# Grouping the query projections of an attention-and-FFN kernel into bursts of eight heads

## The chip, the cores and the metric

The kernel runs on one core of a Trainium2 chip. The metric is the device time of one execution, in microseconds. A profile of one more execution was taken beside the timed runs; its instructions carry start times, so a reader can follow each engine. In the rows PE is TensorE (PEld its weight loads), DVE is VectorE, ACT is ScalarE, POOL is GpSimd and SP is the engine that issues most transfers.

## The reference

One block computes `x + s * silu(ffn)` from a layer-normed input `xn` of 2048 rows by 448 columns.

- Attention `s`: `q = xn @ wq` gives 16 query heads of 256 columns; there are 8 key/value heads, each shared by two neighbouring query heads. Only the last 512 keys of the cache are used (W = 512). Per head: scores `q k^T / 16`, softmax over 512 keys, times `v`; the 16 heads side by side (4096 columns) go through `wo` (4096 x 448).
- FFN: `(gelu(xn @ w_gate) * (xn @ w_up)) @ w_down` with 1792 hidden columns, then silu.

All inputs and the output are bf16.

## The kernel before

The rows are cut into 4 chunks of 512 (`NQC`), each of 4 tiles of 128 (`TPC`). First comes the FFN, chunk by chunk (`gate_up`, `down`); the last chunk's `down` is interleaved into the start of attention. Its result stays in SBUF as `gy`.

Attention is one loop over 64 steps `i` (4 chunks times 16 heads), each with four tiles `t`. The order in which TensorE gets its work is written out by hand in that loop:

- `scores(i, t)`: two matmuls (L420) into PSUM bank 4 or 5 in turn; ScalarE takes the exponential with a row sum (L424) into a ring of bf16 tiles `pr`; VectorE takes the reciprocal (L426) and scales the tile (L427); SP issues a transposing transfer into `pT[i % 4]` (issued at L236). The ring has 9 tiles.
- `values(i, e_)`: four matmuls (L440) of `V` with the transposed head, one group for each half `e_` of the 256 columns, at even `t`. VectorE casts the result into `oT` (L446; ScalarE does so for the last two heads, L448). The PSUM banks come from a list of eight, `(0, 6, 0, 6, 0, 1, 6, 6)`, walked group by group; it is lined up so that heads 3, 7, 11, ... use bank 6 for both groups.
- `outproj(G, t, part)`: four heads `G` of one row tile times `wo`, eight matmuls (L460), half of them at `t` = 1 and half at `t` = 3. VectorE adds the result into `acc` (L481). After a chunk's last group POOL multiplies by `gy` and adds the x tile `xr` (L485, L487) and the chunk is stored.
- `q_burst(G)`: the query projections of four heads, 56 matmuls (L406). The contraction is 448 = 7 x 64, so a matmul uses 64 of the 128 rows of the array and two run side by side. ScalarE copies the result into `qT` (L410), two heads at a time, through banks 0 to 3. A burst comes at `t` = 0 of every fourth head, right behind that slot's value group.
- `silu(n)`: a tanh on ScalarE (L499) and two products on POOL (L500, L502), for one of 16 row tiles, behind heads 7, 10, 13, ...

Values trail the scores: the first group runs at head 2, tile 2, so a head's two groups run two heads later at `t` = 2 and three heads later at `t` = 0. Output groups begin at head 6. Behind the loop stand what is left of values and output groups, in the order of a string (`"vvovovv"`, v for values, o for an output group), and the last four output tiles.

Every engine's list of operations is in the program's order, and a small recorder (`Rec`) puts in a semaphore wait where an operation reads or rewrites what another engine or a transfer holds. Buffers of attention lie over those of the FFN, which are dead by then.

Of the kernel before, what the change touches and what calls it, by code (L numbers as in the profile page):

```python
# [5 lines left out]
ACT = mybir.ActivationFunctionType  # L6
ALU = mybir.AluOpType
BF16 = mybir.dt.bfloat16
# [3 lines left out]
P = 128  # L12
# [129 lines left out]
def bass_recurrent_scan__sliding_block_cached__geglu_ffn__prompt_kernel(nc, A_x, A_k, A_v, A_wq, A_wo, B_x, B_wg, B_wu, B_wd, out):  # L142
    _, S, D = A_x.shape
    Hkv, Sk, Dh = A_k.shape[1], A_k.shape[2], A_k.shape[3]
    HD = A_wq.shape[1]
    Hq = HD // Dh
# [4 lines left out]
    NT = NQC * TPC  # L151
# [7 lines left out]
    with es:  # L159
        off = [16512]  # L160

        def sb(name, shape, dt, at=None):
            n = 4 if dt == F32 else 2
            for x in shape[1:]:
                n *= x
            if at is None:
                at = off[0]
                off[0] += (n + 31) // 32 * 32
            return R.place(name, shape, dt, at), at + (n + 31) // 32 * 32
# [24 lines left out]
        hb, ffn_end = sb("hb", [P, NHB, QC], BF16)  # L194


        NPT = 4
        qT, at = sb("qT", [P, 6, NE, QC], BF16, gu_at)
        oT = [None, None]
        oT[0], at = sb("oT0", [P, 4 * NE, QC], BF16, at)  # L200
        xr, at = sb("xr", [P, TPC, D], BF16, at)
        assert at <= x_at
        pT, at = sb("pT", [P, NPT, NJ, QC], BF16, x_at)
        pr = []
        while at + 2 * W <= d_at:
            t_, at = sb("pr%d" % len(pr), [P, W], BF16, at)
            pr.append(t_)
        at = hb_at
        while at + 2 * W <= ffn_end:
            t_, at = sb("pr%d" % len(pr), [P, W], BF16, at)  # L210
            pr.append(t_)
        NPR = len(pr)
        oT[1], at = sb("oT1", [P, 4 * NE, QC], BF16, d_at)
        acc, at = sb("acc", [P, TPC, D], F32, at)
        tmp, at = sb("tmp", [P, 2, D], F32, at)
        ofin, at = sb("ofin", [P, TPC, D], BF16, at)
        assert at <= hb_at, (at, hb_at)
# [175 lines left out]
        NI = NQC * Hq  # L393
        NG = NI // 4

        def q_burst(G):

            c, h0 = divmod(4 * G, Hq)
            for n in range(4):
                hp, e_ = divmod(n, 2)  # L400
                s, i = 2 * (n % 2) if G else (4, 0, 2, 0)[n], (4 * G + 2 * hp) % 6

                def run(e, hp=hp, e_=e_, s=s):
                    for k in range(NK):
                        for b, lo in ((s, 0), (s + 1, HP)):
                            ins = e.matmul(bank(b), lhsT=wq[lo:lo + HP, k, h0 // 2 + hp, e_ * P:(e_ + 1) * P],  # L406
                                           rhs=xnT[lo:lo + HP, c, k, :], start=k == 0, stop=k == NK - 1)
                    return ins
                pe(run, r=xn(c) + [("wq", lo, k) for lo in range(2) for k in range(NK)], w=[("ps", s), ("ps", s + 1)])
                act(lambda e, e_=e_, s=s, i=i: e.activation(  # L410
                    qT[:, i:i + 2, e_, :], psum[:, s * 512:(s + 2) * 512].rearrange("p (a q) -> p a q", a=2), ACT.Copy),
                    r=[("ps", s), ("ps", s + 1)], w=[("qT", i, e_), ("qT", i + 1, e_)])

        def scores(i, t):
            g, n = (i % Hq) // 2, i * TPC + t
            b, s = 4 + n % 2, n % NPR

            def run(e):
                for k in range(NE):
                    ins = e.matmul(bank(b), lhsT=qT[:, i % 6, k, t * P:(t + 1) * P], rhs=kT[:, g, k, :],  # L420
                                   start=k == 0, stop=k == NE - 1)
                return ins
            pe(run, r=[("kT", g), ("qT", i % 6, 0), ("qT", i % 6, 1)], w=[("ps", b)])
            act(lambda e: e.activation(pr[s][:, :], bank(b), ACT.Exp, scale=scale, accum_out=den[:, s:s + 1]),  # L424
                r=[("ps", b)], w=[("pr%d" % s,), ("den", s)])
            dve(lambda e: e.reciprocal(rden[:, s:s + 1], den[:, s:s + 1]), r=[("den", s)], w=[("rden", s)])  # L426
            dve(lambda e: e.tensor_scalar(pr[s][:, :], pr[s][:, :], rden[:, s:s + 1], None, op0=ALU.mult),  # L427
                r=[("pr%d" % s,), ("rden", s)], w=[("pr%d" % s,)])
            dmaT(pT[:, i % NPT, :, t * P:(t + 1) * P], pr[s][:, :], r=[("pr%d" % s,)], w=[("pT", i % NPT, t)], lane="p%d" % s)

        def values(i, e_):
            g = (i % Hq) // 2
            idx = (i % 4) * NE + e_
            at = 2 * i + e_ + 5

            b = (0, 6, 0, 6, 0, 1, 6, 6)[at % 8] if at < 2 * NI else (0, 6, 0, 6, 1)[at - 2 * NI]

            def run(e):
                for j in range(NJ):
                    ins = e.matmul(bank(b), lhsT=V[:, j, g, e_ * P:(e_ + 1) * P], rhs=pT[:, i % NPT, j, :],  # L440
                                   start=j == 0, stop=j == NJ - 1)
                return ins
            pe(run, r=[("pT", i % NPT, t) for t in range(TPC)] + [("V", j) for j in range(NJ)], w=[("ps", b)])
            dst, key = oT[(i // 4) % 2][:, idx, :], ("oT%d" % ((i // 4) % 2), idx)
            if i < NI - 2:
                dve(lambda e: e.tensor_copy(dst, bank(b)), r=[("ps", b)], w=[key])  # L446
            else:
                act(lambda e: e.activation(dst, bank(b), ACT.Copy), r=[("ps", b)], w=[key])  # L448

        def outproj(G, t, part, half=None):  # L450

            n8 = 4 * NE
            lo, hi = (0, D) if half is None else (half * D // 2, (half + 1) * D // 2)
            b = ((2, 2), (3, 5), (7, 4), (0, 6))[t][half or 0] if G == NG - 1 else (7, 7, 7, 4)[t] if G == NG - 2 else 7
            c, h0 = divmod(4 * G, Hq)
            end = c == NQC - 1

# [10 lines left out]
            if end and h0 == Hq - 4:  # L468
                dve(lambda e: e.tensor_tensor(tmp[:, t % 2, lo:hi], bank(b, D)[:, lo:hi], gy[:, n, lo:hi], ALU.mult),  # L469
                    r=[("ps", b), ("gy", n)], w=[("tmp", t % 2)])  # L470
                dve(lambda e: e.tensor_tensor(ofin[:, t, lo:hi], tmp[:, t % 2, lo:hi], acc[:, t, lo:hi], ALU.add),  # L471
                    r=[("tmp", t % 2), ("acc", t)], w=[("ofin", t, lo)])
                if t == TPC - 1:
                    dma("sync" if half else "scalar", o_view[:, c, t, lo:hi], ofin[:, t, lo:hi], r=[("ofin", t, lo)])
                elif half != 0:
                    dma("sync", o_view[:, c, t, :], ofin[:, t, :], r=[("ofin", t, 0), ("ofin", t, lo)])
                return
            if h0 == 0:
                dve(lambda e: e.tensor_copy(acc[:, t, :], bank(b, D)), r=[("ps", b)], w=[("acc", t)])
# [1 line left out]
                dve(lambda e: e.tensor_tensor(acc[:, t, :], bank(b, D), acc[:, t, :], ALU.add),  # L481
                    r=[("ps", b), ("acc", t)], w=[("acc", t)])
            if h0 == Hq - 4 or end and h0 == Hq - 8:
                dst, key = (acc, ("acc", t)) if end else (ofin, ("ofin", t))
                pool(lambda e: e.tensor_tensor(tmp[:, t % 2, :], acc[:, t, :], gy[:, n, :], ALU.mult),  # L485
                     r=[("acc", t), ("gy", n)], w=[("tmp", t % 2)])
                pool(lambda e: e.tensor_tensor(dst[:, t, :], tmp[:, t % 2, :], xr[:, t, :], ALU.add),  # L487
                     r=[("tmp", t % 2), ("xr",)], w=[key])
                if t == TPC - 1 and not end:
                    dma("gpsimd", o_view[:, c, :, :], ofin[:, :, :], r=[("ofin", t) for t in range(TPC)])  # L490
                    load_xr(c + 1)

        def load_xr(c):
            dma("gpsimd", xr[:, :, :], x_view[:, c, :, :], w=[("xr",)])

        def silu(n):

# [26 lines left out]
        q_burst(0)  # L524
        load_xr(0)

        fill = {}
# [5 lines left out]
        for i in range(NI):  # L533
            for t in range(TPC):
                scores(i, t)
                if 4 * i + t in fill:
                    down(NQC - 1, *fill[4 * i + t])
                if t % 2 == 0 and 4 * i + t >= 10:
                    values(*pv.pop(0))
                if 6 <= i and t % 2:  # L540
                    outproj(*outs[0], range(2 * t - 2, 2 * t + 2))
                    if t == TPC - 1:
                        outs.pop(0)
                if t == 0 and i % 4 == 3 and i + 1 < NI:
                    q_burst(i // 4 + 1)
            if 7 <= i and (i - 7) % 3 == 0 and (i - 7) // 3 < NT:
                silu((i - 7) // 3)

        for what in "vvovovv":
            if what == "v":  # L550
                values(*pv.pop(0))
            else:
                outproj(*outs.pop(0), range(4 * NE))
# [36 lines left out]
```

## Time and profile before

| | |
|---|---|
| median of 3 runs | 560.89 us (560.74 to 561.54) |
| the profiled execution, whole | 561.18 us |
| its span, first to last instruction | 559.4 us |
| TensorE busy | 549.0 us (98%) |
| VectorE, ScalarE, POOL busy | 322.9, 296.1, 90.1 us |
| granted TensorE clock | 1.00 throughout |
| FFN and layer norm | up to about 126.7 us |
| attention loop | about 126.7 to 542.4 us |

Matmuls are pipelined: the profile gives one of 512 columns 379 ns, but the next one starts after about 216 ns. So on TensorE the rows are best read by their starts, and a hole is a start that comes later than the work before it explains. A few matmul records are missing from the trace (481 of 512 score matmuls are there, 510 of 512 value matmuls), which looks like a hole of 216 ns and is none.

### The profile page before, as it was taken

The numbers are of one execution on the slowest core, as the hardware profiler recorded it, in microseconds if no ns is written. First come the engines' busy times: TensorE is split into PE (matmuls) and PEld (weight loads), VectorE is DVE, ScalarE is ACT, GpSimd is POOL, SyncE is SP. The second block draws the span as 40 slices with busy tenths as digits, with TensorE's granted clock in tenths as the row PEclk, the third lists the DMA queues.
The fourth block names the chain that finished last, engine by engine and source line by source line (L and its number), as shares of the span: only waits on it lengthen the run. The fifth ranks groups of instructions, "written<-read, shape, count | busy, mean of one in ns | idle before, by whom it ended". The sixth has DMA issues, their size and how long they took to land.

```text
span 559.4 us, 9865 instructions
## 1 busy us (share of the span) xinstructions
PE 549.0 (98%) x3499; PEld 257.2 (46%) x3532; DVE 322.9 (58%) x835; ACT 296.1 (53%) x673; POOL 90.1 (16%) x125
## 2 busy tenths in 40 slices
PE   7999999999999999999999999999999999999997
PEld 3544444444444444444444444444444444444445
DVE  5636446143464847474846657484747484755674
ACT  4324233247655565556565656656565656565641
POOL 0232323200000111013501101232100021400023
PEclk9999999999999999999999999999999999999999
DMA  8994746972453435353664344445535353645352
GB/s 193 276 191 86 138 102 136 247 137 65 94 85 68 97 64 99 69 91 64 143 98 94 73 86 71 81 84 137 101 67 99 63 95 71 147 79 101 70 92 52
DMA packets 169552, 58.83 MB, mean 105 GB/s; under 512 B 160160, under 2 KB 166432, under 8 KB 169504
## 3 DMA queue, kind: packets, MB, share of 16 engines
q1 hardware_dynamic: 166208, 45.50, 44.2%
q0 software_dynamic: 3152, 12.65, 8.9%
q8 instruction: 28, 0.46, 0.4%
q14 instruction: 20, 0.16, 0.1%
q10 hardware_dynamic: 144, 0.06, 0.0%
HBM read 17.92 MB, written 1.84 MB: 35 GB/s over the span
## 4 chain that ended last, share of the span: by engine, by line
PE 95%; DMA 1%; DVE 1%; issue 1%; SPq 1%; ACT 0%
PE ps L440 20%; PE ps L420 19%; PE ps L406 18%; PE ps L460 16%; PE ps L370 15%; PE ps L382 8%; DMA wgu<-in_B_w_up_dram 1%; SPq L233 1%; DVE tmp L469 0%; DVE ofin L471 0%; DVE pr L427 0%; DVE oT L446 0%; DVE rden L426 0%; ACT pr L424 0%
## 5 line engine op out<-in xcount | busy, mean ns | idle before, releaser
L424 ACT ACTIVATE pr<-ps 128x512 bf16<-128x512 f32 x256 | 152.8, 597 | 116.6 <-PE ps L420 112.5
L420 PE MATMUL ps<-kT,qT 128*128 128x512 bf16 x481 | 145.4, 379 | 3.3 <-issue 2.5
L440 PE MATMUL ps<-pT,V 128*128 128x512 bf16 x510 | 130.8, 379 | 0.6 <-DVE rden L426 0.4
L426 DVE RECIPROCAL rden<-den 128x1 f32<-128x1 f32 x256 | 41.5, 162 | 152.4 <-ACT pr L424 134.3
L460 PE MATMUL ps<-wo,oT 128*128 128x448 bf16 (+1 forms) x536 | 116.3, 344 | 0.0
L427 DVE TENSOR_SCALAR pr<-pr,rden 128x512 bf16<-128x512 bf16 x256 | 106.4, 416 | 9.0
L406 PE MATMUL ps<-xnT,wq 64*128 64x512 bf16 x896 | 99.5, 376 | 0.0
L410 ACT ACTIVATE qT<-ps 128x1024 bf16<-128x1024 f32 x64 | 65.5, 1024 | 49.8 <-PE ps L406 49.8
L370 PE MATMUL ps<-xnT,wgu 64*128 64x512 bf16 x784 | 85.5, 376 | 1.0 <-ACT xnT L322 0.8
L446 DVE CAST oT<-ps 128x512 bf16<-128x512 f32 x124 | 84.6, 682 | 0.6 <-PE ps L440 0.5
L440 PEld LDWEIGHTS ps<-pT,V 128*128 128x128 bf16 x512 | 49.9, 98 | 60.8 <-issue 1.2
L460 PEld LDWEIGHTS ps<-wo,oT 128*128 128x128 bf16 x536 | 52.3, 98 | 51.1
L420 PEld LDWEIGHTS ps<-kT,qT 128*128 128x128 bf16 x512 | 48.5, 98 | 57.1 <-issue 7.3
L376 DVE TENSOR_TENSOR actT<-ps,hb 128x512 bf16<-128x512 f32 x56 | 38.1, 685 | 57.5 <-ACT hb L374 55.7
L406 PEld LDWEIGHTS ps<-xnT,wq 64*128 64x128 bf16 x896 | 42.4, 94 | 55.9 <-DVE acc L481 4.2
L374 ACT ACTIVATE hb<-ps 128x512 bf16<-128x512 f32 x56 | 33.4, 597 | 51.8 <-PE ps L370 51.8
L370 PEld LDWEIGHTS ps<-xnT,wgu 64*128 64x128 bf16 x784 | 39.2, 94 | 46.5 <-issue 2.5
L424 ACT ACTIVATION_READ_ACCUMULATOR pr<-ps 128x1 f32 x256 | 49.9, 195 | 0.0
L500 POOL TENSOR_SCALAR tmp<-tmp 128x448 f32<-128x448 f32 x16 | 9.1, 572 | 233.9 <-ACT tmp L499 233.9
L382 PE MATMUL ps<-wd,actT 128*128 128x448 bf16 x224 | 46.2, 353 | 0.1
L485 POOL TENSOR_TENSOR tmp<-acc,gy 128x448 f32<-128x448 f32 x16 | 16.6, 1035 | 123.2 <-DVE acc L481 123.2
L382 PEld LDWEIGHTS ps<-wd,actT 128*128 128x128 bf16 x224 | 21.7, 98 | 22.2 <-issue 1.3
(43 smaller groups left out, 171.7 us busy)
## 6 DMA issues: line engine op xcount, KB each, us to landing
pT<-pr SPq DMA_TRANSPOSE x256, 2.4
wq<-in_A_wq_dram POOLq DMA_DIRECT2D x14, 256.0 KB, 4.3
wo<-in_A_wo_dram POOLq DMA_DIRECT2D x4, 896.0 KB, 10.1
V<-in_A_v_cache_dram POOLq DMA_DIRECT2D x4, 512.0 KB, 5.8
xr<-in_A_x_dram POOLq DMA_DIRECT2D x4, 448.0 KB, 4.8
wd<-in_B_w_down_dram SPq DMA_DIRECT2D x1, 1568.0 KB, 17.6
wgu<-in_B_w_gate_dram SPq DMA_DIRECT2D x3, 448.0 KB, 10.3
wgu<-in_B_w_up_dram SPq DMA_DIRECT2D x3, 448.0 KB, 11.8
```

The lines of the kernel that those rows point to most:

```text
L370: ins = e.matmul(bank(b), lhsT=wgu[lo:lo + HP, k, f * P:(f + 1) * P], rhs=xnT[lo:lo + HP, c, k, :], start=k == 0, stop=k == NK - 1)
L376: dve(lambda e: e.tensor_tensor(actT[:, f, :], bank(s + 1), hb[:, n % NHB, :], ALU.mult), r=[("ps", s + 1), ("hb", n % NHB)], w=[("actT", f)])
L382: pe(lambda e, f=f: e.matmul(bank(b, D), lhsT=actT[:, f, t * P:(t + 1) * P], rhs=wd[:, f, :], start=f == 0, stop=f == NF - 1), r=[("actT", ...
L406: ins = e.matmul(bank(b), lhsT=wq[lo:lo + HP, k, h0 // 2 + hp, e_ * P:(e_ + 1) * P], rhs=xnT[lo:lo + HP, c, k, :], start=k == 0, stop=k == ...
L410: act(lambda e, e_=e_, s=s, i=i: e.activation(qT[:, i:i + 2, e_, :], psum[:, s * 512:(s + 2) * 512].rearrange("p (a q) -> p a q", a=2), AC ...
L420: ins = e.matmul(bank(b), lhsT=qT[:, i % 6, k, t * P:(t + 1) * P], rhs=kT[:, g, k, :], start=k == 0, stop=k == NE - 1)
L424: act(lambda e: e.activation(pr[s][:, :], bank(b), ACT.Exp, scale=scale, accum_out=den[:, s:s + 1]), r=[("ps", b)], w=[("pr%d" % s,), ("de ...
L426: dve(lambda e: e.reciprocal(rden[:, s:s + 1], den[:, s:s + 1]), r=[("den", s)], w=[("rden", s)])
L427: dve(lambda e: e.tensor_scalar(pr[s][:, :], pr[s][:, :], rden[:, s:s + 1], None, op0=ALU.mult), r=[("pr%d" % s,), ("rden", s)], w=[("pr%d ...
L440: ins = e.matmul(bank(b), lhsT=V[:, j, g, e_ * P:(e_ + 1) * P], rhs=pT[:, i % NPT, j, :], start=j == 0, stop=j == NJ - 1)
L446: dve(lambda e: e.tensor_copy(dst, bank(b)), r=[("ps", b)], w=[key])
L460: ins = e.matmul(bank(b, D)[:, lo:hi], lhsT=oT[G % 2][:, idx, t * P:(t + 1) * P], rhs=wo[:, h0 * NE + idx, lo:hi], start=idx == 0, stop=id ...
```

## The change

- Queries are projected in bursts of four heads at heads 0 and 3, and from head 7 on in bursts of eight, at heads 7, 15, 23, ... 55. `qT` becomes five buffers of two heads each, three in the old place and two in the dead FFN area.
- Values begin at head 3, tile 0: both groups of a head now run three heads behind its scores. The list of banks keeps its place relative to the loop's steps.
- Output groups begin at head 7 in place of 6. Behind the loop stand one value group and one output group more (`"vvovovovv"`).
- The gate's tanh and products run behind heads 7, 9, 11 and 13 of each chunk.
- `ofin` is gone: the result is written over the x tile `xr`. The ring `pr` has 10 tiles.

```diff
+        NPT, NQP = 4, 5
+        qT = [None] * NQP
...
+        def q_slot(i):
+            p = i // 2
+            p = p if p < 3 else (p - 3) % NQP
+            return qT[p], "qT%d" % p, i % 2
...
-        def q_burst(G):
-            c, h0 = divmod(4 * G, Hq)
-            for n in range(4):
+        def q_burst(i0, heads):
+            c, h0 = divmod(i0, Hq)
+            for n in range(heads):
                 hp, e_ = divmod(n, 2)
-                s, i = 2 * (n % 2) if G else (4, 0, 2, 0)[n], (4 * G + 2 * hp) % 6
+                s = 2 * (n % 2) if i0 else (4, 0, 2, 0)[n]
+                buf, name, _ = q_slot(i0 + 2 * hp)
...
-            at = 2 * i + e_ + 5
-            b = (0, 6, 0, 6, 0, 1, 6, 6)[at % 8] if at < 2 * NI else (0, 6, 0, 6, 1)[at - 2 * NI]
+            at = 2 * i + e_ + 6
+            b = (0, 6, 0, 6, 0, 1, 6, 6)[at % 8] if at < 2 * NI else (0, 6, 1, 0, 6, 1)[at - 2 * NI]
...
-            b = ((2, 2), (3, 5), (7, 4), (0, 6))[t][half or 0] if G == NG - 1 else (7, 7, 7, 4)[t] if G == NG - 2 else 7
+            b = ((2, 2), (3, 5), (4, 7), (0, 6))[t][half or 0] if G == NG - 1 else (7, 7, 4, 7)[t] if G == NG - 2 else 7
...
-                dst, key = (acc, ("acc", t)) if end else (ofin, ("ofin", t))
+                dst, key = (acc, ("acc", t)) if end else (xr, ("xr", t))
...
-                if t % 2 == 0 and 4 * i + t >= 10:
+                if t % 2 == 0 and 4 * i + t >= 12:
                     values(*pv.pop(0))
-                if 6 <= i and t % 2:
+                if 7 <= i and t % 2:
                     outproj(*outs[0], range(2 * t - 2, 2 * t + 2))
                     if t == TPC - 1:
                         outs.pop(0)
-                if t == 0 and i % 4 == 3 and i + 1 < NI:
-                    q_burst(i // 4 + 1)
-            if 7 <= i and (i - 7) % 3 == 0 and (i - 7) // 3 < NT:
-                silu((i - 7) // 3)
-        for what in "vvovovv":
+                if t == 0 and (i == 3 or i % 8 == 7) and i + 1 < NI:
+                    q_burst(i + 1, 4 if i == 3 else 8)
+            if i % Hq in (7, 9, 11, 13):
+                silu(i // Hq * TPC + (i % Hq - 7) // 2)
+        for what in "vvovovovv":
```

More of the change, by code (lines that the diff above doesn't have):

```diff
@@ L194, in bass_recurrent_scan__sliding_block_cached__geglu_ffn__prompt_kernel, with fill_pr @@
         hb, ffn_end = sb("hb", [P, NHB, QC], BF16)
-        NPT = 4
-        qT, at = sb("qT", [P, 6, NE, QC], BF16, gu_at)
+        NPT, NQP = 4, 5
+        qT = [None] * NQP
         oT = [None, None]
+        at = gu_at
+        for n in range(3):
+            qT[n], at = sb("qT%d" % n, [P, 2, NE, QC], BF16, at)
         oT[0], at = sb("oT0", [P, 4 * NE, QC], BF16, at)
         xr, at = sb("xr", [P, TPC, D], BF16, at)
-        assert at <= x_at
-        pT, at = sb("pT", [P, NPT, NJ, QC], BF16, x_at)
[L204 to L212, printed above, removed]
+        pr = []
+        def fill_pr(at, end):
+            while at + 2 * W <= end:
+                t_, at = sb("pr%d" % len(pr), [P, W], BF16, at)
+                pr.append(t_)
+        fill_pr(at, x_at)
+        pT, at = sb("pT", [P, NPT, NJ, QC], BF16, x_at)
+        fill_pr(at, d_at)
         oT[1], at = sb("oT1", [P, 4 * NE, QC], BF16, d_at)
@@ L215, in bass_recurrent_scan__sliding_block_cached__geglu_ffn__prompt_kernel @@
         tmp, at = sb("tmp", [P, 2, D], F32, at)
-        ofin, at = sb("ofin", [P, TPC, D], BF16, at)
-        assert at <= hb_at, (at, hb_at)
+        for n in range(3, NQP):
+            qT[n], at = sb("qT%d" % n, [P, 2, NE, QC], BF16, at)
+        assert at >= hb_at, (at, hb_at)
+        fill_pr(at, nc.sbuf_usable_end)
+        NPR = len(pr)
         psum = es.enter_context(nc.psum_tensor("ps", [P, 8 * 512], F32))
@@ L409, in q_burst @@
                 pe(run, r=xn(c) + [("wq", lo, k) for lo in range(2) for k in range(NK)], w=[("ps", s), ("ps", s + 1)])
-                act(lambda e, e_=e_, s=s, i=i: e.activation(
-                    qT[:, i:i + 2, e_, :], psum[:, s * 512:(s + 2) * 512].rearrange("p (a q) -> p a q", a=2), ACT.Copy),
-                    r=[("ps", s), ("ps", s + 1)], w=[("qT", i, e_), ("qT", i + 1, e_)])
+                act(lambda e, e_=e_, s=s, buf=buf: e.activation(
+                    buf[:, :, e_, :], psum[:, s * 512:(s + 2) * 512].rearrange("p (a q) -> p a q", a=2), ACT.Copy),
+                    r=[("ps", s), ("ps", s + 1)], w=[(name, e_)])
         def scores(i, t):
@@ L416, in scores @@
             b, s = 4 + n % 2, n % NPR
+            buf, name, a = q_slot(i)
             def run(e):
                 for k in range(NE):
-                    ins = e.matmul(bank(b), lhsT=qT[:, i % 6, k, t * P:(t + 1) * P], rhs=kT[:, g, k, :],
+                    ins = e.matmul(bank(b), lhsT=buf[:, a, k, t * P:(t + 1) * P], rhs=kT[:, g, k, :],
                                    start=k == 0, stop=k == NE - 1)
                 return ins
-            pe(run, r=[("kT", g), ("qT", i % 6, 0), ("qT", i % 6, 1)], w=[("ps", b)])
+            pe(run, r=[("kT", g), (name, 0), (name, 1)], w=[("ps", b)])
             act(lambda e: e.activation(pr[s][:, :], bank(b), ACT.Exp, scale=scale, accum_out=den[:, s:s + 1]),
@@ L470, in outproj @@
                     r=[("ps", b), ("gy", n)], w=[("tmp", t % 2)])
-                dve(lambda e: e.tensor_tensor(ofin[:, t, lo:hi], tmp[:, t % 2, lo:hi], acc[:, t, lo:hi], ALU.add),
-                    r=[("tmp", t % 2), ("acc", t)], w=[("ofin", t, lo)])
+                dve(lambda e: e.tensor_tensor(xr[:, t, lo:hi], tmp[:, t % 2, lo:hi], acc[:, t, lo:hi], ALU.add),
+                    r=[("tmp", t % 2), ("acc", t)], w=[("xr", t, lo), ("xr", t)])
                 if t == TPC - 1:
-                    dma("sync" if half else "scalar", o_view[:, c, t, lo:hi], ofin[:, t, lo:hi], r=[("ofin", t, lo)])
+                    dma("sync" if half else "scalar", o_view[:, c, t, lo:hi], xr[:, t, lo:hi], r=[("xr", t, lo)])
                 elif half != 0:
-                    dma("sync", o_view[:, c, t, :], ofin[:, t, :], r=[("ofin", t, 0), ("ofin", t, lo)])
+                    dma("sync", o_view[:, c, t, :], xr[:, t, :], r=[("xr", t, 0), ("xr", t, lo)])
                 return
@@ L487, in outproj @@
                 pool(lambda e: e.tensor_tensor(dst[:, t, :], tmp[:, t % 2, :], xr[:, t, :], ALU.add),
-                     r=[("tmp", t % 2), ("xr",)], w=[key])
+                     r=[("tmp", t % 2), ("xr", t)], w=[key])
                 if t == TPC - 1 and not end:
-                    dma("gpsimd", o_view[:, c, :, :], ofin[:, :, :], r=[("ofin", t) for t in range(TPC)])
+                    dma("gpsimd", o_view[:, c, :, :], xr[:, :, :], r=[("xr", t) for t in range(TPC)])
                     load_xr(c + 1)
         def load_xr(c):
-            dma("gpsimd", xr[:, :, :], x_view[:, c, :, :], w=[("xr",)])
+            dma("gpsimd", xr[:, :, :], x_view[:, c, :, :], w=[("xr", t) for t in range(TPC)])
         def silu(n):
@@ L523, in bass_recurrent_scan__sliding_block_cached__geglu_ffn__prompt_kernel @@
         act(lambda e: e.activation(small[:, 2:3], small[:, 0:1], ACT.Exp), r=[("eps",)], w=[("warm",)])
-        q_burst(0)
+        q_burst(0, 4)
         load_xr(0)
```

## The prediction

> **What bounds the kernel now.** I read the page's head first, then the chain of work that ended last.
>
> ```profile
> span 559.4 us, 9865 instructions
> ...
> PE 549.0 (98%) x3499; PEld 257.2 (46%) x3532; DVE 322.9 (58%) x835; ACT 296.1 (53%) x673; POOL 90.1 (16%) x125
> ...
> PEclk9999999999999999999999999999999999999999
> ...
> PE 95%; DMA 1%; DVE 1%; issue 1%; SPq 1%; ACT 0%
> ```
>
> TensorE carries 95% of the chain at an undiminished clock, so only two things can move the time: holes in TensorE's stream, and the few microseconds at head and tail. The next view is TensorE's own timeline across one query burst.
>
> ```profile
> 352.13 1.03 PE L440 MATMUL ps<-pT,V 128*128 128x512 bf16 x4
> 352.99 0.59 PE L420 MATMUL ps<-kT,qT 128*128 128x512 bf16 x2
> 353.42 0.92 PE L460 MATMUL ps<-wo,oT 128*128 128x448 bf16 x4
> 354.18 0.59 PE L420 MATMUL ps<-kT,qT 128*128 128x512 bf16 x2
> 354.61 1.03 PE L440 MATMUL ps<-pT,V 128*128 128x512 bf16 x4
> 355.57 6.22 PE L406 MATMUL ps<-xnT,wq 64*128 64x512 bf16 x56
> 361.95 0.38 PE L420 MATMUL ps<-kT,qT 128*128 128x512 bf16 x1 [0.16 <-issue]
> ```
>
> Go by starts, since ends are modelled. Four value matmuls take 352.99 - 352.13 = 0.86 us; ahead of the burst the same four are followed only after 0.96. That is 0.10 us for entering the 64-row form. At the exit one score record is missing (x1 where there are two, 0.22 us), so scores began at 361.73; 28 pairs at 0.216 from 355.57 end at 361.61: 0.12 more. The period confirms it: two score tiles with one output part and one value group repeat every 2.484 us (S); eight of them and the burst are 19.87 + 6.04 = 25.91, and bursts are 26.12 apart: **0.21 us per burst**. The crossings of gate/up and down show 93 to 96 ns too, with other producers on either side, so I read it as the price of changing form, not as a wait for someone.
>
> The last view is the tail, engines together.
>
> ```profile
> 538.60 0.96 DVE L427 TENSOR_SCALAR pr<-pr,rden 128x512 bf16<-128x512 bf16 x1
> ...
> 539.48 0.68 DVE L446 CAST oT<-ps 128x512 bf16<-128x512 f32 x1
> ...
> 540.52 0.81 PE L440 MATMUL ps<-pT,V 128*128 128x512 bf16 x3 [0.40 <-DVE rden L426]
> ...
> 541.16 0.59 PE L420 MATMUL ps<-kT,qT 128*128 128x512 bf16 x2
> ...
> 542.35 1.89 PE L440 MATMUL ps<-pT,V 128*128 128x512 bf16 x8
> 544.08 1.68 PE L460 MATMUL ps<-wo,oT 128*128 128x448 bf16 x8
> ...
> 546.45 1.68 PE L460 MATMUL ps<-wo,oT 128*128 128x448 bf16 x8
> 548.29 1.89 PE L440 MATMUL ps<-pT,V 128*128 128x512 bf16 x8 [0.15 <-issue]
> ```
>
> Two holes: 0.34 us at 540 (the row lacks one record) and 0.32 at 548.29 (the output group ends 546.45 + 1.51 = 547.96). The first: head 63's two value groups both use PSUM bank 6; the cast that empties it ended at 540.16, late because the scaling before it took 0.96 instead of 0.35 beside a POOL product; the matmul followed 0.14 later. The second: the last tile's transpose.
>
> ```profile
> L236 SPq DMA_TRANSPOSE pT<-pr x256: 1188/1216/2334, 135.2 to 545.6; - x128
> ```
>
> SP takes 1.22 us for an issue and starts one every 1.311 us when it is behind, but TensorE makes a tile every S/2 = 1.242. So in a run without a burst SP falls behind; in the burst it catches up. The last tile was scaled at 543.06, issued at 545.60 (a lag of 2.54) and used at 548.29, 2.68 after its issue.
>
> **The change part by part.**
>
> *Bursts of eight.* Bursts fall from 16 to 9. The work in them is the same, so 7 x 0.21 = **1.47 us** go, directly from TensorE's stream. Inside a longer burst ScalarE must empty two banks in 1.02 us (L410) per 14 pairs of 1.51 us: 0.49 spare, as now, and each unit finds its banks free. The queries written are of pairs not being scored (five buffers, one pair in use, four written): no wait. Cover gone, it would cost up to 1.02 per unit, but before shows none in the 30 units that reuse banks.
>
> *Values three heads behind.* They need the fourth tile of their head. Tile to value was 7 steps and a score group (9.1 us), becomes 9 steps (11.6). Subtract 1.90 (score start to scaled tile) and 2.68: the lag that is tolerated rises from 4.5 to 7.0 us. Largest lag now: 3.75. In eight heads without a burst SP's slower pace brings the lag to 2.7, and slow issues add to it: 12 of 256 took over 2 us, each about 1.0 above the usual, some 21 us apart; issues beside POOL's transfers cost up to 1.3 in a run. That is 4.7 to 6.0 ahead of the burst. Values that run before that burst need at most the 23rd tile after the last one, where the lag is 3.0 to 5.3. Under 7.0: **0**. The scaled-tile ring grows from 9 to 10 (8.7 us of lag allowed): 0. Four transposed heads still suffice: a slot's values end two steps before its rewrite begins.
>
> *Head 63.* Its POOL product moves behind the last tile, so the late cast goes: **-0.34**.
>
> *Tail.* One value group (0.86) and one output group (1.51) move from the loop to behind the last score: no work more, but the last transpose gets that much more cover. Values of head 63 may start on TensorE 0.43 + 0.76 + 4 x 0.864 + 3 x 1.51 = 9.17 us after the last score's start; on SP's side 1.90 + lag + 2.68. TensorE waits once the lag passes 4.59. The run since the last burst is now 35 tiles (heads 55 to 63), not 19: SP needs 34 x 1.311 = 44.6 us, the tiles come in 41.8, so the lag is 2.8 without slow issues, 5.8 with three. At one per 21 us in 45 us I take two: 4.9 with 0.1 of small change, and a wait of 0.3 instead of 0.32 + 2.37 of less cover. From both sides: 0 and 1.2. So the hole at 548 stays nearly as it was: -0.32 + 0.30 = **-0.02**.
>
> SP's slow issues lie beside the packets of one instruction queue, 16 KB each, which come about every 250 of TensorE's 7031 instructions:
>
> ```profile
> q8 instruction: 28, 0.46, 0.4%
> ```
>
> The page "Runtime: NRT & Kernel Launch", section Instruction fetch mechanics, says that code is refilled in 16 KiB blocks of 256 instructions and that crossing a boundary is mostly hidden. By that rule the lag would stay at 2.8 and the hole would close (558.8 us). The rows here show a refill that is not hidden from SP, and the sum goes by them.
>
> *Bank 6 twice.* Heads 3 (mod 4) use bank 6 for both value groups. Now a burst stands between; after, heads 11, 19, ... 59 have none, 7 of them. An undisturbed cast ends 2.07 us after its value group began, and the next may start 0.14 later, at 2.21 against 2.484: 0.27 spare, **0**. A scaling beside POOL adds 0.61 and makes 0.34 of wait (the one seen). POOL's products follow the head before: gate tangents now disturb heads 8, 10, 12, 14 (mod 16), the chunk's outputs heads 20 to 23 and so on. None is 11, 19, 27...
>
> *The rest.* Output a head later: 0 (POOL's last chunk output has over 10 us before its next work). The result is written over the x tile, so POOL's reload of x queues behind the output transfer (4.3 us landing); behind it wait only gate products of the next head, and POOL is idle for tens of microseconds: 0. If that cover went, a gate product would be late for an output nine or more heads off. Head 6 has no output part, 0.86 us a tile against ScalarE's 0.62 pace: 0, at worst 0.2.
>
> **Sum.** -1.47 - 0.34 - 0.02 = -1.83 us on the profiled execution (561.18 in all, span 559.4), which lies 0.29 above the median of the runs; the difference carries over: 560.89 - 1.83 = **559.1**.
>
> **The rivals.**
>
> *SP's queue ends the kernel.* If three slow issues fall in the last 35 tiles, the lag is 5.8 and the wait 1.2: -1.81 - 0.32 + 1.2 = -0.93, 560.0, within 0.2%. For: in the trace slow issues at tiles 224 and 254 both lie in this stretch. Against: the spacing. Chance 0.24.
>
> *Bank 6 makes it slower.* One mechanism: at the seven heads the cast comes late again. Decides once it is more than 0.27 late; at the measured 0.61 it costs 7 x 0.34 = 2.4, giving 561.4; slower than 0.2% from 0.42 per head, that is casts 0.69 late; 0.76 per head at 1.03 late, a whole POOL product, gives 560.89 - 1.83 + 5.3 = 564.4. I take 562.9. For: the hole at 540. Against: POOL's order above. The page "SBUF — State Buffer", Who interferes with whom, calls the shared port an exclusive lock in which the loser blocks for the whole instruction. The trace shows 0.61 of a 1.03 us product; by the rule this rival's upper end would hold, by the row the lower. Chance 0.09.
>
> *The 0.21 is not per burst* but a wait that grows with the burst: only -0.36 remains, 560.5. Against: 15 entries and six other crossings agree within 4 ns. Chance 0.05.
>
> **How the numbers follow.** The forecast case has 0.62, with its own range of 558.5 to 559.6 (tail wait 0 to 0.6, 0.2 of scatter). Adding SP's case: 558.5 to 560.4. A difference under 0.2%, 1.1 us, is what a measurement of this kernel cannot tell from none. Faster 0.66: the forecast and the mildest of SP's case; same 0.26: the rest of SP's, the third rival, a mild bank case; slower 0.08.
>
> **What would show it.** Right: 8-head bursts about 52.0 us apart (51.82 + 0.21); no hole over 0.1 us between the bursts; the wait at 540 gone; last scores some 4.2 us earlier at about 537.0, and the last values at about 546.4. Wrong: idle at L453 in heads 11, 19, ... (bank 6); the last values at 547 or later with SP's last issue over 4.6 us behind its tile; TensorE waiting inside the burst for L422's evictions.

## The result, and the profile after

| | before | after |
|---|---|---|
| median of the runs | 560.82 us (560.61 to 561.54, 6 runs) | 558.72 us (558.64 to 559.05, 6 runs) |
| the profiled execution, whole | 561.18 us | 558.75 us |
| its span | 559.4 us | 557.0 us |
| up to the first query matmul (FFN, layer norm) | 126.69 us | 126.31 us |
| first query matmul to start of the last matmul | 429.34 us | 427.29 us |

The ratio is 0.9962 [0.9949, 0.9975]: 0.4% faster, beyond the 0.2% that a measurement can tell, and 0.4 us below the forecast of 559.1. In the new code scores, values, output and queries are the lines L433, L453, L473 and L418 (before: L420, L440, L460 and L406).

The last two rows of the table split the 2.4 us between the two profiled executions. The 0.37 us ahead of attention isn't the change's: before had a hole of 0.38 us at 12 us, where TensorE waited for a weight transfer, and this execution had none. Attention itself became **2.05 us** shorter. The page of the changed kernel:

```profile
span 557.0 us, 9857 instructions
...
PE 548.7 (99%) x3498; PEld 258.8 (46%) x3532; DVE 324.1 (58%) x835; ACT 296.3 (53%) x673; POOL 89.7 (16%) x125
...
PEclk9999999999999999999999999999999999999999
...
PE 97%; DVE 2%; issue 1%; DMA 0%; ACT 0%
```

TensorE's busy time and clock are what they were; its share of the chain rose from 95% to 97%, and SPq is gone from it. So nothing became quicker: holes closed. TensorE's waits (line waited at, what for, us in total, times, longest) show which. In the kernel before they had these two rows:

```profile
PE ps L420 <- issue: 2.5, 16, 0.2
...
PE ps L440 <- DVE rden L426: 0.4, 1, 0.4
```

In the changed kernel the first of them, the exits from the bursts, occurs 9 times instead of 16, and the second has no counterpart left:

```profile
PE ps L433 <- issue: 1.4, 9, 0.2
```

TensorE's timeline across a burst of eight heads in the changed kernel:

```profile
324.66 0.59 PE L433 MATMUL ps<-kT,qT 128*128 128x512 bf16 x2
325.09 1.03 PE L453 MATMUL ps<-pT,V 128*128 128x512 bf16 x4
326.05 12.26 PE L418 MATMUL ps<-xnT,wq 64*128 64x512 bf16 x112
338.47 0.38 PE L433 MATMUL ps<-kT,qT 128*128 128x512 bf16 x1 [0.16 <-issue]
```

By starts, the entry is 326.05 - 325.09 - 0.86 = 0.10 us, the same as ahead of a burst of half the length, and the 112 matmuls run through without an idle row of their own. The burst before this one starts at 274.02 and the one behind it at 378.09: 52.03 us apart both times. The last stretch of the stream:

```profile
535.71 1.03 PE L453 MATMUL ps<-pT,V 128*128 128x512 bf16 x4
536.79 0.38 PE L433 MATMUL ps<-kT,qT 128*128 128x512 bf16 x1
537.00 0.92 PE L473 MATMUL ps<-wo,oT 128*128 128x448 bf16 x4
537.76 1.89 PE L453 MATMUL ps<-pT,V 128*128 128x512 bf16 x8
539.49 1.68 PE L473 MATMUL ps<-wo,oT 128*128 128x448 bf16 x8
...
544.24 1.68 PE L473 MATMUL ps<-wo,oT 128*128 128x448 bf16 x8
545.86 1.89 PE L453 MATMUL ps<-pT,V 128*128 128x512 bf16 x7
547.58 6.28 PE L473 MATMUL ps<-wo,oT 128*128 128x448 bf16 x56
```

The last scores are those at 536.57 and 536.79 (one record is missing). Behind them everything follows without a hole up to 544.24 + 1.51 = 545.75; the last values start at 545.86, 0.10 us late. SP's row of the changed kernel:

```profile
L241 SPq DMA_TRANSPOSE pT<-pr x256: 1188/1216/2472, 134.8 to 543.3; - x128
```

The last tile was scaled at 538.48 and issued at 543.28: a lag of 4.80 us, against 2.54 before. So the lag nearly doubled, as the change's longer stretch without a burst makes it, and the extra value and output groups behind the loop took it up almost exactly.

### The profile page after: what moved, and what is told of

Same layout as the page of the kernel before. It is cut to its first block, busy times and chain, and to the rows that moved or that the text cites. A ratio compares the mean times of both kernels' runs of the same rounds, so it can differ in the third digit from the quotient of the medians.

```text
span 557.0 us, 9857 instructions
## 1 busy us (share of the span) xinstructions
PE 548.7 (99%) x3498; PEld 258.8 (46%) x3532; DVE 324.1 (58%) x835; ACT 296.3 (53%) x673; POOL 89.7 (16%) x125
## 4 chain that ended last, share of the span: by engine, by line
PE 97%; DVE 2%; issue 1%; DMA 0%; ACT 0%
PE ps L453 20%; PE ps L433 20%; PE ps L418 18%; PE ps L473 17%; PE ps L375 15%; PE ps L387 8%; DVE tmp L482 0%; DVE xr L484 0%; DVE stats L293 0%; DMA x<-in_A_x_dram 0%; PE ps L321 0%; ACT xnT L327 0%; DVE mv L294 0%; DVE xn L299 0%; DVE rstd L338 0%
## 5 line engine op out<-in xcount | busy, mean ns | idle before, releaser
L433 PE MATMUL ps<-kT,qT 128*128 128x512 bf16 x493 | 147.7, 379 | 2.0 <-issue 1.4
L453 PE MATMUL ps<-pT,V 128*128 128x512 bf16 x497 | 129.1, 379 | 0.8
L439 DVE RECIPROCAL rden<-den 128x1 f32<-128x1 f32 x256 | 41.5, 162 | 148.2 <-ACT pr L437 129.8
L473 PE MATMUL ps<-wo,oT 128*128 128x448 bf16 (+1 forms) x536 | 116.2, 344 | 0.0
L440 DVE TENSOR_SCALAR pr<-pr,rden 128x512 bf16<-128x512 bf16 x256 | 108.0, 422 | 9.0
L418 PE MATMUL ps<-xnT,wq 64*128 64x512 bf16 x896 | 98.3, 376 | 0.0
L459 DVE CAST oT<-ps 128x512 bf16<-128x512 f32 x124 | 84.5, 682 | 0.7 <-PE ps L453 0.5
L453 PEld LDWEIGHTS ps<-pT,V 128*128 128x128 bf16 x512 | 50.0, 98 | 60.2 <-issue 0.3
L473 PEld LDWEIGHTS ps<-wo,oT 128*128 128x128 bf16 x536 | 52.4, 98 | 51.0
L433 PEld LDWEIGHTS ps<-kT,qT 128*128 128x128 bf16 x512 | 49.1, 98 | 55.8 <-issue 4.5
L418 PEld LDWEIGHTS ps<-xnT,wq 64*128 64x128 bf16 x896 | 43.0, 94 | 54.6 <-DVE acc L494 2.5
```

Source lines behind the costliest of these rows:

```text
L433: ins = e.matmul(bank(b), lhsT=buf[:, a, k, t * P:(t + 1) * P], rhs=kT[:, g, k, :], start=k == 0, stop=k == NE - 1)
L473: ins = e.matmul(bank(b, D)[:, lo:hi], lhsT=oT[G % 2][:, idx, t * P:(t + 1) * P], rhs=wo[:, h0 * NE + idx, lo:hi], start=idx == 0, stop=id ...
```

## The experiments

All edits are to the changed kernel. Times are medians with their range, ratios are to the kernel before. "Attention" is the stretch of the table's last row, 427.29 us in the changed kernel; it is the better measure where few tenths matter, as the next run shows.

**The changed kernel again.** No edit: a second measurement beside other kernels.

> The changed kernel itself, unaltered, beside the same runs of the kernel before: its attention part should again take 427.3 us from the first query matmul to the last matmul, with a hole of 0 to 1 us ahead of the last values, and its time lie 2 us below the kernel before. If the FFN part, which left holes of 0.4 to 2.4 us in single profiles, is what makes runs differ, a second profile shows another FFN part and the same attention part.

Measured: 558.97 us (558.75 to 559.53), 0.9962 [0.9947, 0.9976]. The profiled execution took 559.53 us, 0.78 more than the first one. Its part ahead of attention is 0.87 us longer (127.18), its attention 0.10 us shorter (427.19): the last tile's lag was 3.75 us, and the hole ahead of the last values is gone. So the part ahead of attention differs between two executions by some two fifths of what the change brings, while attention differs only by the hole in the tail, which goes with the lag. (That hole can be larger: two executions of a kernel shown below, with lags of 3.53 and 4.77 us, differ by 1.0 us in attention.)

**Many small bursts: is it the crossing, or the length?** Each eight-head burst becomes four of two heads, at the same head's four steps.

```diff
-                if t == 0 and (i == 3 or i % 8 == 7) and i + 1 < NI:
-                    q_burst(i + 1, 4 if i == 3 else 8)
+                if t == 0 and i == 3:
+                    q_burst(i + 1, 4)
+                if i % 8 == 7 and i + 1 < NI:
+                    q_burst(i + 1 + 2 * t, 2)
```

> The changed kernel, but each burst of eight heads is cut into four pieces of two heads, run at tiles 0, 1, 2 and 3 of the same head, with scores, values and outputs between them. The work and the order of the heads are the same; 21 more crossings into the 64-row form and back. Theory (0.21 us for each pair of crossings, whatever stands beside it): 21 x 0.21 = 4.4 us more than the changed kernel, 558.7 + 4.4 = 563.1 us, and in the trace 0.096 us at each entry and 0.10 at each exit. Rival (the 0.21 is a wait that a burst pays once, or that grows with its length): 558.7 us or at most 1.5 more.

Measured: 564.34 us (563.45 to 565.17), 1.0056 [1.0042, 1.0069]; attention 432.68, 5.39 longer. TensorE's timeline of this kernel at one of the new pieces:

```profile
331.28 0.60 PE L433 MATMUL ps<-kT,qT 128*128 128x512 bf16 x2
331.72 0.92 PE L473 MATMUL ps<-wo,oT 128*128 128x448 bf16 x4
332.58 3.19 PE L418 MATMUL ps<-xnT,wq 64*128 64x512 bf16 x28
335.93 0.38 PE L433 MATMUL ps<-kT,qT 128*128 128x512 bf16 x1 [0.16 <-issue]
```

The entry is 332.58 - 331.72 - 0.76 = 0.10, now behind output matmuls instead of values and with a burst of a quarter of the length. Over the kernel each entry is 95 to 96 ns; each exit is 116 to 117 ns, counted up to the second score matmul, with 215.8 ns for a pair of the burst. The remainder of the 5.39 is in the tail, as TensorE's waits of this kernel say:

```profile
PE ps L433 <- issue: 2.5, 16, 0.2
PE ps L453 <- DMA pT<-pr: 0.9, 1, 0.9
```

The last tile's lag was 5.73 us and the hole ahead of the last values 1.04, 0.94 more than in the changed kernel. 5.39 - 0.94 = 4.45 for 21 further pairs of crossings: 0.21 each, which is what entry and exit come to. The price goes with the number of crossings and not with the work between them; the prediction's third rival falls. The 0.94 I had not expected.

**Bursts of four, all else changed.** This undoes the longer burst alone.

```diff
-                if t == 0 and (i == 3 or i % 8 == 7) and i + 1 < NI:
-                    q_burst(i + 1, 4 if i == 3 else 8)
+                if t == 0 and i % 4 == 3 and i + 1 < NI:
+                    q_burst(i + 1, 4)
```

> The changed kernel with bursts of four heads at every fourth head again; all else stays changed. Theory: seven pairs of crossings come back, 7 x 0.21 = 1.47 us, and the last run without a burst is 19 tiles in place of 35, so the hole of 0.10 us ahead of the last values goes: 558.7 + 1.4 = 560.1 us. Rival (the gain came from the later values, outputs and gate products): 558.7 us.

Measured: 560.74 us (560.22 to 564.16), 0.9998 [0.9985, 1.0011]; attention 428.68, 1.39 longer, without any hole in the tail. With the 0.10 of the changed kernel's tail that is 1.49 us for 7 pairs of crossings, 0.21 each again. Its profiled execution had a hole ahead of attention, in TensorE's waits:

```profile
PE ps L375 <- DMA xnT<-xn: 1.7, 1, 1.7
```

so the whole execution (562.24 us) says less than its attention. Without the longer bursts the rest of the change brings 0.66 us in attention (429.34 to 428.68), which is the two holes of 0.34 and 0.32, and nothing that the median tells.

**The gate ahead of the heads that use bank 6 twice.** The prediction's second rival said that a cast beside a POOL product would make those heads late, and that only the new places of the gate keep POOL away. This puts the gate's products where they meet them. The list holds 16 heads; seven of them are followed by a head of the sort 11, 19, ... 59. (These heads are steps of the loop: the value groups that run there belong to the heads two or three steps back.)

```diff
+        gate_at = [7, 10, 13, 18, 23, 26, 29, 34, 39, 42, 45, 50, 55, 57, 58, 61]
...
-            if i % Hq in (7, 9, 11, 13):
-                silu(i // Hq * TPC + (i % Hq - 7) // 2)
+            if i in gate_at:
+                silu(gate_at.index(i))
```

> The changed kernel, with the gate's tanh and products behind heads 10, 18, 26, 34, 42, 50, 58 and nine others, so that POOL's products fall into the first tile of heads 11, 19, ... 59, which use PSUM bank 6 for both value groups with no burst between. Theory: at each of the seven the cast ends 0.61 us later and TensorE waits 0.34: 558.7 + 2.4 = 561.1 us. If a product blocked VectorE for its whole 1.03 us: 7 x 0.76 = 5.3, 564.0 us. Rival (where the gate products stand is of no matter): 558.7 us.

Measured: 561.01 us (560.61 to 562.57), 1.0002 [0.9992, 1.0012]; attention 429.05, 1.76 longer, and the tail without a hole. TensorE's waits of this kernel:

```profile
PE ps L453 <- DVE rden L439: 2.2, 7, 0.3
```

Seven waits, 1.87 us together by starts: 0.27 each, where I expected 0.34. The engines together at head 11 show the chain:

```profile
203.75 1.03 POOL L515 TENSOR_TENSOR gy<-tmp,gy 128x448 bf16<-128x448 f32 x1
...
203.97 0.96 DVE L440 TENSOR_SCALAR pr<-pr,rden 128x512 bf16<-128x512 bf16 x1
...
204.86 0.68 DVE L459 CAST oT<-ps 128x512 bf16<-128x512 f32 x1
...
205.59 0.55 PEld L453 LDWEIGHTS ps<-pT,V 128*128 128x128 bf16 x4 [0.58 <-DVE oT L459]
```

POOL's product begins, VectorE's scaling begins 0.22 later and ends at 204.93, 0.15 after the product's end at 204.78; undisturbed it takes 0.35. The cast follows and TensorE's next value group waits for it. The releaser in the waits is named as L439; the weight loads' row names the cast, L459, which is the one that empties the bank. The rule that I weighed in the prediction ("SBUF — State Buffer", Who interferes with whom) says that whoever issues first has the shared pair of ports for its whole instruction and the other blocks fully. I had taken it to ask for a delay of a whole product; it asks only for a wait until the product has ended, and the rows agree: with 0.81 us of the product left the scaling took 0.96, and elsewhere in the changed kernel, with 0.26 left, 0.41. Each time it ended 0.15 after the product. So it lost 0.61 of a 1.03 us product here.

The scaling lost the same 0.61 us at 540 in the kernel before, and the cast ended 2.68 us after its value group had begun both times. What differs is the step from the cast to the next value matmul: 0.15 us there, 0.07 here. That is the 0.34 against 0.27; why the step differs stays open.

**The same gate, with one bank of the list changed.** If the late cast costs only because both groups of such a head share a bank, another bank takes the cost away though POOL still disturbs.

```diff
+        gate_at = [7, 10, 13, 18, 23, 26, 29, 34, 39, 42, 45, 50, 55, 57, 58, 61]
...
-            b = (0, 6, 0, 6, 0, 1, 6, 6)[at % 8] if at < 2 * NI else (0, 6, 1, 0, 6, 1)[at - 2 * NI]
+            b = (0, 6, 0, 6, 0, 1, 6, 1)[at % 8] if at < 2 * NI else (0, 6, 1, 0, 6, 1)[at - 2 * NI]
```

> As the run with the gate products ahead of heads 11, 19, ... 59, but the second value group of those heads goes to bank 1 in place of bank 6. POOL's and VectorE's work is the same. Theory (the wait is for the bank): the seven waits go, 558.7 us. Rival (it is VectorE's or POOL's load as such): as that run, about 561.1 us.

Measured: 559.18 us (558.99 to 566.15), 0.9974 [0.9954, 0.9995]; attention 427.19, and no wait at L453 in the view of waits. That is the changed kernel with neither gain nor loss. The shared bank was the condition, POOL's product the trigger. The prediction's second rival was therefore a true mechanism that this kernel's order of heads avoids.

**Output a head earlier.** The prediction gave "output a head later" a price of 0 and didn't ask whether it is needed. This leaves the values three heads behind and lets output begin at head 6 as before.

```diff
-            b = ((2, 2), (3, 5), (4, 7), (0, 6))[t][half or 0] if G == NG - 1 else (7, 7, 4, 7)[t] if G == NG - 2 else 7
+            b = ((2, 2), (3, 5), (7, 4), (0, 6))[t][half or 0] if G == NG - 1 else (7, 7, 7, 4)[t] if G == NG - 2 else 7
...
-                if 7 <= i and t % 2:
+                if 6 <= i and t % 2:
...
-        for what in "vvovovovv":
+        for what in "vvovovvv":
```

> The changed kernel with output groups from head 6 in place of 7; values stay three heads behind. Each group's second half then needs a value group that began only 1.30 us before, whose cast ends 2.07 us after that start. Theory (the later outputs are what the later values need): TensorE waits about 0.85 us in 15 heads, 6, 10, ... 62, some 13 us in all, and the pauses let SP catch up, so that the tail has no hole: about 571.5 us. Rival (the edit costs nothing, as the prediction had it, apart from 1.51 us less cover in the tail): a hole of about 1.6 us ahead of the last values, 560.3 us.

Measured: 571.87 us (571.64 to 572.12), 1.0190 [1.0175, 1.0205]; attention 440.09, 12.8 longer. TensorE's waits, and the engines together at head 10, of this kernel:

```profile
PE ps L473 <- DVE oT L459: 10.3, 15, 0.8
```

```profile
201.12 1.03 PE L453 MATMUL ps<-pT,V 128*128 128x512 bf16 x4
...
201.98 0.59 PE L433 MATMUL ps<-kT,qT 128*128 128x512 bf16 x2
...
202.51 0.68 DVE L459 CAST oT<-ps 128x512 bf16<-128x512 f32 x1
...
203.25 0.36 PE L473 MATMUL ps<-wo,oT 128*128 128x448 bf16 x1 [0.67 <-DVE oT L459]
```

An output group needs four heads cast. Values now end later, and the second part of a group's first output tile stands one score tile behind the last value group of its four heads: the scores end at 201.98 + 0.43 = 202.41, the cast at 203.19, and the output matmul starts at 203.25, 0.84 late. At each of 15 output groups that makes 12.6 us, nearly the whole difference. So the shift of values can't do without the shift of output.

**Values two heads behind.** This undoes the shift of values and keeps the rest: bursts of eight and output from head 7.

```diff
-            at = 2 * i + e_ + 6
-            b = (0, 6, 0, 6, 0, 1, 6, 6)[at % 8] if at < 2 * NI else (0, 6, 1, 0, 6, 1)[at - 2 * NI]
+            at = 2 * i + e_ + 5
+            b = (0, 6, 0, 6, 0, 1, 6, 6)[at % 8] if at < 2 * NI else (0, 6, 0, 6, 1)[at - 2 * NI]
...
-                if t % 2 == 0 and 4 * i + t >= 12:
+                if t % 2 == 0 and 4 * i + t >= 10:
...
-        for what in "vvovovovv":
+        for what in "vvovoovv":
```

> The changed kernel with values two heads behind again (first group at head 2, tile 2); bursts of eight, outputs and gate products stay changed. One value group moves from behind the loop into it, so the last values have 0.86 us less cover. The runs so far put the limit at a lag of 4.7 us of SP behind the last scaled tile (4.80 left a hole of 0.10, 5.73 one of 1.04). Theory (in the loop the lag of the tiles that matter, at most 4.3, stays under the 4.5 that two heads allow; only the tail pays): the limit falls to 3.84, and with the lag of 4.8 that the changed kernel showed the hole ahead of the last values is 0.96 us: attention 0.9 us longer, 559.6 us. Rival (eight heads without a burst need the third head of slack all along): holes before the values of heads 4 to 6 of each run, some 0.3 to 1 us in each of seven runs, 561 to 565 us.

Measured: 560.47 us (559.62 to 561.76), 0.9983 [0.9973, 0.9993]; attention 427.31. In this profiled execution the last tile's lag was only 3.53 us, and it shows a hole of 0.12 us between two value groups behind the loop and none inside the loop or ahead of the last values. What makes its 561.76 us long lies ahead of attention (129.27 us until the first query matmul). So this profile showed next to nothing of a price of the tail, though the median is 1.5 us above the changed kernel's in its second measurement (558.97). It was run again beside the changed kernel:

> Values two heads behind once more, now beside the changed kernel on the same chip. The first profile had a lag of 3.53 us at the last tile, under the limit of 3.84, and so no hole, where 0.96 was expected at a lag of 4.8. Theory: no hole in the loop again; in the tail a hole of lag - 3.84, whatever the lag is; over the runs up to 0.9 us more than the changed kernel. Rival (the values' place is of no matter to the time): the same time as the changed kernel within 0.3 us.

Measured: 559.98 us (559.06 to 560.63), 0.9975 [0.9964, 0.9986], 1.0 us above the changed kernel on the same chip (558.97). Now the lag was 4.77 us, and attention 428.33, 1.14 above the changed kernel's run beside it. TensorE's timeline of the tail:

```profile
538.37 0.92 PE L473 MATMUL ps<-wo,oT 128*128 128x448 bf16 x4
539.13 1.03 PE L453 MATMUL ps<-pT,V 128*128 128x512 bf16 x4
541.11 1.02 PE L453 MATMUL ps<-pT,V 128*128 128x512 bf16 x4 [0.96 <-DVE oT L459]
541.97 1.30 PE L473 MATMUL ps<-wo,oT 128*128 128x448 bf16 x6
```

The hole is 541.11 - 539.13 - 0.86 = 1.12 us. I had the size and not the place: with values two heads behind, the group that is late is head 62's, which has still less work ahead of it, and not head 63's. The row names a cast of VectorE; the one that empties this group's bank had ended at 539.15. The start fits head 62's last tile, which SP issued at 538.41, 2.70 us before. In the first of the two runs that tile was issued at 539.88 and its group began at 542.56, 2.68 later. Its lag was 2.55 there, with a hole of 0.12, and 3.53 here, with one of 1.12: lag and hole grew by the same 1.0 us. So values three heads behind buy cover for the last tiles; inside the loop two were enough in both profiles.

**The same groups in the tail, in another order.** To test the tail's limit, head 63's values are put two output groups (3.02 us) nearer.

```diff
-        for what in "vvovovovv":
+        for what in "vvovvvvoo":
```

> The changed kernel with the order behind the loop altered: two output groups that stood ahead of the values of head 63 stand behind them (v v o v v v v o o in place of v v o v o v o v v). The work and the loop are the same; the last transpose has 2 x 1.51 = 3.02 us less cover. Theory (TensorE waits in the tail once SP's lag passes a limit, which falls from 4.7 to 1.7 us): with a lag of 4.8 a hole of 3.1 us ahead of the last values in place of 0.10, 558.7 + 3.0 = 561.7 us; from 3.5 to 5.7 of lag, the spread of the runs so far, 560.5 to 562.7. Rival (the tail's hole has nothing to do with SP): 558.7 us.

Measured: 563.41 us (561.70 to 568.31), 1.0032 [1.0006, 1.0059]; attention 430.30, 3.0 longer. TensorE's timeline of this kernel, and who waits for SP's transposes (us, times):

```profile
541.85 1.89 PE L453 MATMUL ps<-pT,V 128*128 128x512 bf16 x8
546.69 1.89 PE L453 MATMUL ps<-pT,V 128*128 128x512 bf16 x8 [2.95 <-DMA pT<-pr]
548.41 0.92 PE L473 MATMUL ps<-wo,oT 128*128 128x448 bf16 x4
```

```profile
L241 SPq DMA_TRANSPOSE pT<-pr x256: 1188/1216/2663, 135.7 to 544.0; - x128
  PE ps L453: 3.0, 1
```

The hole is 546.69 - 541.85 - 1.73 = 3.11 us at a lag of 4.68. The changed order bears a lag of 4.70: at 4.80 it had a hole of 0.10, at 5.73 (the burst in four pieces) 1.04, at 3.75 none. With 3.02 less cover it should bear 1.68, and 4.68 - 1.68 = 3.0. The 0.1 us between 3.0 and 3.11 is the way from the issue to the first matmul: 546.69 - 544.00 = 2.69 here, 545.86 - 543.28 = 2.58 in the changed kernel. So one straight line holds over these points to 0.1 us: what exceeds the cover is a hole of that length. The time is still 1.7 us above what was expected; 1.1 us of it is behind the last matmul, which lies 4.5 us ahead of the span's end instead of 3.4. That two output groups now end together would explain it; no run shows that.

**More instructions for the same work.** If the packets of the instruction queue slow SP's issues, more packets should make more slow issues. Scores and values are computed in two halves of 256 columns.

```diff
-                for k in range(NE):
-                    ins = e.matmul(bank(b), lhsT=buf[:, a, k, t * P:(t + 1) * P], rhs=kT[:, g, k, :],
-                                   start=k == 0, stop=k == NE - 1)
+                for o in range(0, 512, 256):
+                    for k in range(NE):
+                        ins = e.matmul(bank(b)[:, o:o + 256], lhsT=buf[:, a, k, t * P:(t + 1) * P], rhs=kT[:, g, k, o:o + 256],
+                                       start=k == 0, stop=k == NE - 1)
...
-                for j in range(NJ):
-                    ins = e.matmul(bank(b), lhsT=V[:, j, g, e_ * P:(e_ + 1) * P], rhs=pT[:, i % NPT, j, :],
-                                   start=j == 0, stop=j == NJ - 1)
+                for o in range(0, 512, 256):
+                    for j in range(NJ):
+                        ins = e.matmul(bank(b)[:, o:o + 256], lhsT=V[:, j, g, e_ * P:(e_ + 1) * P], rhs=pT[:, i % NPT, j, o:o + 256],
+                                       start=j == 0, stop=j == NJ - 1)
```

> The changed kernel with every score and value matmul cut into two of 256 columns: the same work, but 2 x 1024 more instructions on TensorE (weight loads and matmuls). Theory (SP's slow issues come with the refills of TensorE's instructions): 28 packets of 16 KB become about 36, and of the 256 transposes those over 1.9 us become about 17 to 19 in place of 11 to 12; more lag, a larger hole in the tail. Rival (the slow issues are SP's own): 11 to 12 stay. The time itself may rise by some microseconds, as twice as many matmuls each carry their start.

Measured, in one execution: 562.96 us, attention 430.33. The row of the instruction queue (packets, MB, share) became

```profile
q8 instruction: 36, 0.59, 0.5%
```

against 28 packets in the changed kernel: 8 more for 2048 more instructions, as expected. Issues of a transposed tile over 1.9 us: 16, fewer than the 17 to 19 expected, against 11 in the changed kernel and 7 to 16 in the others with 28 packets. By itself that count decides nothing. The last tile's lag was 5.35 us and the hole ahead of the last values 0.61, which the limit of 4.70 puts at 0.65.

When the slow issues happen says more: over all twelve profiles of this study, 133 of the 134 issues over 1.9 us overlap a packet of that queue in time, and 80 of the 2810 under 1.3 us do. Seen from the packets, 185 meet an issue of a transposed tile, and only 6 of these meet none but issues under 1.3 us. It is a coincidence in time in every profile; that the packet is the cause is not shown. The page "Runtime: NRT & Kernel Launch", section Instruction fetch mechanics, calls the crossing into a new block mostly hidden. TensorE bears that out: in the second run of the changed kernel its only holes in attention are those at the 64-row form's crossings and two near 153 us, of 0.22 and 0.03 us, where no packet is. SP doesn't: 133 of the 185 packets go with about 1 us on an issue.

## Why the prediction was right

**Bursts of eight, -1.47.** Right in size and cause. The 0.21 us is paid per pair of crossings, whatever work stands ahead of it (values or outputs) and however long the burst (2, 4 or 8 heads): 21 pairs more cost 4.45, 7 pairs more cost 1.49. (One figure beside it is misread, without effect on the sum: the 1.51 us of a unit of the burst are 14 matmuls, that is 7 pairs and not 14.) In the second run of the changed kernel the records around one burst are complete:

```profile
482.06 1.03 PE L453 MATMUL ps<-pT,V 128*128 128x512 bf16 x4
483.02 12.26 PE L418 MATMUL ps<-xnT,wq 64*128 64x512 bf16 x112
495.21 0.61 PE L433 MATMUL ps<-kT,qT 128*128 128x512 bf16 x2
```

The entry is 0.10 us. For the exit the pair's time is needed to one more digit: bursts of 56 and of 112 matmuls take 5.842 and 11.885 us from their first start to their last, so 28 pairs take 6.043, and one 0.2158. The first score matmul then starts 495.21 - 483.02 - 56 x 0.2158 = 0.11 late, and the second one 0.01 more: together the 0.12 of the prediction and, with the entry, its 0.21. What TensorE does in that time no run shows.

**Head 63, -0.34.** Right: the wait at L440 <- L426 is gone, and no other took its place.

**Tail, -0.02.** The term that was mis-sized, by 0.20: the hole fell from 0.32 to 0.10, not to 0.30. The lag was foreseen to 0.1 us (4.80 for 4.9, with the two slow issues that I took). What was off was the limit, 4.70 and not 4.59, because the values started 2.58 us after the last issue and not 2.68, and the same 0.1 again in the lag. That the lag came out so near is partly luck: it goes with the number of slow issues (over 1.9 us) among the last 35 tiles. In the eight profiles that end on 35 tiles without a burst (leaving out the one with output a head earlier, where TensorE's waits let SP catch up) it was 3.5 to 4.2 us with one, 4.7 to 4.8 with two and 5.35 with three. Of the two executions of the changed kernel the first had two and the second had one. With the measured hole the sum is 1.47 + 0.34 + 0.22 = 2.03 of the 2.05 us measured in attention; the rest of the difference to the profile before, 0.37 us, is a transfer ahead of attention that came earlier and was no part of the prediction.

**Bank 6, 0.** Right, and for the reason given: in the changed kernel the second value group of heads 11, 19, ... 59 starts 2.48 us after the first, without a wait. Where POOL was made to meet them, it cost 0.27 each and not 0.34: the scaling lost the 0.61 of the prediction, but the matmul followed its cast 0.07 us later and not 0.15. The upper end of this rival, a delay of a whole product, rested on a misreading of the page: no scaling lost more than what was left of the product. At 0.27 the rival's price is 7 x 0.27 = 1.9 us, enough to end at no difference (561.0 measured), not slower.

**SP's queue ends the kernel.** The rival's mechanism is real and came within 0.1 us of showing. Its condition is the number of slow issues in the last 35 tiles, and that differs between executions: the lag was 4.80 with two and 3.75 with one in two executions of the changed kernel. In the burst in four pieces there were three, and the lag was 5.73, with a hole of 1.04 where the rival had foretold 1.2 at 5.8.

**Values three heads behind, 0; output a head later, 0.** Both right as times of the whole change, and here the reasoning was incomplete. I looked for what the shifts disturb and found nothing. I didn't ask what they are for. Without the later output the later values would have cost 12.8 us, six times the gain; without the later values the tail costs up to 1.1 us. The lag inside the loop, which I compared with 7.0, was at most 4.25 and 4.27 in the two profiles of the changed kernel for heads whose values run before the next burst, under the 4.5 that was tolerated before: in these executions the loop didn't need the change. The margin is less than one slow issue, so another execution may need it.

**The signs named beforehand.** Bursts 52.0 apart: 52.03. Last scores at 537.0 and last values at 546.4: 536.57 and 545.86, or 536.9 and 546.2 with the 0.37 us of the earlier start put back.

## What to carry to other kernels

Price a break in a uniform instruction stream by itself, from the starts on both sides of it, and ask how many breaks the order needs: here nothing but their number counted. When two stages are shifted together, price each shift without the other, because a shift that costs nothing may be the one that keeps its neighbour from costing much more. And for a queue that falls behind in a long uniform stretch, compare its lag at the last item with the work that stands ahead of that item's use: what exceeds it is the hole, to a tenth of a microsecond.

## What the runs showed of the hardware

- A change of TensorE between the 128-row and the 64-row form costs 0.096 us on the way in and 0.12 on the way out, behind values and behind outputs, and for bursts of 2, 4 and 8 heads.
- SP's issues that took about 1 us longer than usual coincide with packets of the instruction queue (133 of 134, against 80 of 2810 among the short ones). Whether the packet delays the issue, and how, stays open: no run took the packets away.
- VectorE's scaling that begins beside a POOL product ends 0.15 us after the product: with 0.81 us of the product left it takes 0.96, with 0.26 left 0.41, and 0.35 undisturbed.
- The part ahead of attention, which no kernel here altered, took 126.3 to 129.3 us in the twelve profiles. In the two longest, TensorE's longest wait there is for a transfer into `xnT` (1.7 and 2.2 us). So a difference of 2 us in the whole time needs the stretch's own time beside it.
